# Pooled attention and a gelu layer on one core: v pooled over 128 partitions, its last pools moved by matmuls, and the first batch and the loads put in a new order

## The chip, the cores and the metric

The kernel runs on one core of one Trainium2 chip. The metric is the device time of one launch in microseconds (us), the median of several runs. The profile's own span of an execution is some 1.8 us shorter than the time that is reported for it. Each run has a state: slow when it is over 1.5% above the fastest of the same kernel, otherwise fast. All runs that are compared here ran in the fast state; the one execution that did not is named where it occurs.

## The reference, cut to what matters

Keys and values are averaged over 8 neighbouring positions, 576 positions to 72 pools. Attention goes to these 72 pools, and a two-layer network with a gelu follows. There are 8 batches of 8 heads with 64 columns each.

```python
k_p = k.reshape(B, H, Sp, pool, D).mean(axis=3)     # B 8, H 8, Sp 72, pool 8, D 64
v_p = v.reshape(B, H, Sp, pool, D).mean(axis=3)
scores = scale * np.matmul(q, k_p.transpose(0, 1, 3, 2))
attn = softmax(scores)                              # written out in the original
x = np.matmul(attn, v_p)                            # as 4608 tokens x 512
h = x @ w_in                                        # 512 x 2048
out = gelu_tanh(h) @ w_out                          # 2048 x 512
```

Inputs and output are f32; the kernel multiplies in bf16.

## The kernel before

The 4608 tokens are worked through in 9 groups of 512. Each group has a first phase (64 matmuls with w_in, then gelu on ScalarE) and a second phase (64 matmuls with w_out). The attention of batch g+1 is woven into the second phase of group g. The attention of batch 0 has nothing to hide behind and runs first.

v is put on 72 partitions, one for each pool. It is loaded in 64 partitions and 8 partitions where SyncE issues it:

```python
def load_v(b, eng, h0=0, h1=H):
    ...
    rows = v[b, h0:h1].rearrange("h (j l) d -> j h (l d)", l=8)
    for j0, j1 in ((0, 64), (64, Sp)) if eng is nc.sync else ((0, Sp),):
        eng.dma_start(out=vs[b][j0:j1, h0:h1], in_=rows[j0:j1])
```

k is put on 128 partitions of 4 pools each, and the 64 pools that are left over fill half of a fifth column (`KR`). Pooling is three halving adds on VectorE. The loads are issued in this order: k, v, q of batch 0; two quarters of w_in; k and q of batch 1; two more quarters of w_in; w_out; and v of batch 1 by SyncE in the middle of batch 0's attention.

Batch 0 runs head pair by head pair, and the first 16 matmuls of the first phase are split: their left 288 columns are done inside batch 0's attention.

```python
early = [(fo, ko) for ko in range(KO) for fo in range(4)]
take = (0, 0, 0, 0, 0, 4, 6, 6)
for i, (c, pr) in enumerate(ORDER):
    bank = (4, 6, 0, 2, 4, 6, 4, 6)[i]
    av(0, c, pr, bank)       # outputs and denominators
    norm(0, c, pr, bank)     # Ln, Exp of -1 times it: the inverse
    mult(0, c, pr, bank)
    if i == 3:
        ...
        load_v(1, nc.sync)
    for fo, ko in early[:take[i]]:
        p1_mm(0, fo, ko, 0, CH)
    early = early[take[i]:]
```

PE (TensorE, which does the matmuls) also runs "spins", matmuls on a tile of zeros, where it would stand still. A value matmul below is one that multiplies the exponentials with the pooled v.

The softmax here doesn't subtract the row's maximum and nothing guards it: scores larger than these inputs give would overflow.

Of the kernel before, what the change touches and what calls it, by code (L numbers as in the profile page):

```python
# [18 lines left out]
def kernel(  # L19
# [29 lines left out]
    kvp = ctx.enter_context(tc.tile_pool(name="kvp", bufs=2))  # L49
# [12 lines left out]
    vs, qs = {}, {}  # L62
    kts = [consts.tile([128, KR + 1, 512], F32, name=f"kt{i}") for i in range(2)]

    def load_k(b, engs):
        rows = k[b].rearrange("h (j l) d -> (h j) (l d)", l=8)
        main = rows[0:128 * KR].rearrange("(p r) c -> p r c", r=KR)
        n = KR // len(engs)
        for i, eng in enumerate(engs):
            eng.dma_start(out=kts[b % 2][:, i * n:(i + 1) * n], in_=main[:, i * n:(i + 1) * n])  # L70
        engs[-1].dma_start(out=kts[b % 2][64:128, KR], in_=rows[128 * KR:])

    def load_v(b, eng, h0=0, h1=H):
        if b not in vs:
            vs[b] = kvp.tile([Sp, H, 512], F32, name="vt")
        rows = v[b, h0:h1].rearrange("h (j l) d -> j h (l d)", l=8)

        for j0, j1 in ((0, 64), (64, Sp)) if eng is nc.sync else ((0, Sp),):
            eng.dma_start(out=vs[b][j0:j1, h0:h1], in_=rows[j0:j1])
# [8 lines left out]
    w_in_b = consts.tile([128, KO, DF], BF16, name="w_in_b")  # L88
    w_out_b = consts.tile([128, FO, DM], BF16, name="w_out_b")
    w_in_v = moe_w_in.rearrange("(ko p) f -> p ko f", p=128)  # L90
    w_out_v = moe_w_out.rearrange("(fo p) d -> p fo d", p=128)
# [4 lines left out]
    load_v(0, nc.sync, 0, 4)  # L96
    load_v(0, nc.sync, 4, 8)
# [4 lines left out]
    def load_w_in(i):  # L102
        nc.gpsimd.dma_start(out=w_in_b[:, :, i * 512:(i + 1) * 512], in_=w_in_v[:, :, i * 512:(i + 1) * 512])  # L103

    load_w_in(0)
    load_w_in(1)

# [3 lines left out]
    kTs = [consts.tile([128, 2, H, Sp], BF16, name=f"kT{i}") for i in range(2)]  # L111
    kps = [consts.tile([128, KR + 2, D], BF16, name=f"kp{i}") for i in range(2)]

    vps = [consts.tile([Sp, PR, 2, 2, D], BF16, name=f"vp{i}") for i in range(2)]

    vz = consts.tile([Sp, PR, 2, 2, D], BF16, name="vz")
    ones = consts.tile([Sp, 2, 2, D], BF16, name="ones")
    gate = consts.tile([1, 2], BF16, name="gate")
    idle = consts.tile([128, 512], BF16, name="idle")
    nc.vector.memset(idle, 0.0)  # L120
    nc.vector.memset(kts[0][0:64, KR], 0.0)
    nc.vector.memset(kps[0], 0.0)
    nc.vector.memset(kTs[0], 0.0)
    nc.vector.memset(vz, 0.0)
    nc.vector.memset(ones, 0.0)
    nc.vector.memset(ones[:, 0, 0], 8.0)
    nc.vector.memset(ones[:, 1, 1], 8.0)
    nc.gpsimd.memset(kTs[1], 0.0)  # L128
    nc.gpsimd.memset(kps[1], 0.0)
    nc.gpsimd.memset(kts[1][0:64, KR], 0.0)  # L130
    nc.gpsimd.memset(vps[0], 8.0)  # L131
    nc.gpsimd.memset(vps[1], 8.0)  # L132

    load_k(1, [nc.gpsimd])
    load_q(1)
    load_w_in(2)
    load_w_in(3)
    for i in range(4):
        nc.gpsimd.dma_start(out=w_out_b[:, 4 * i:4 * i + 4, :], in_=w_out_v[:, 4 * i:4 * i + 4, :])
# [7 lines left out]
    def k_steps(b):  # L147

        t = kts[b % 2]
        return [lambda: add(t[:, :, 0:256], t[:, :, 0:256], t[:, :, 256:512]),  # L150
                lambda: add(t[:, :, 0:128], t[:, :, 0:128], t[:, :, 128:256]),
                lambda: add(kps[b % 2][:, 0:KR + 1], t[:, :, 0:64], t[:, :, 64:128])]

    def v_steps(b, hf):
        t = vs[b][:, hf * 4:(hf + 1) * 4]

        def s3():
            w = (vps[b % 2] if b else vz)[:, 2 * hf:2 * hf + 2]
            for e in range(2):
                add(w[:, :, e, e, :], t[:, e::2, 0:64], t[:, e::2, 64:128])  # L160

        return [lambda: add(t[:, :, 0:256], t[:, :, 0:256], t[:, :, 256:512]),
                lambda: add(t[:, :, 0:128], t[:, :, 0:128], t[:, :, 128:256]), s3]
# [4 lines left out]
    def trans_k(b, bank, odd_eng=None):  # L168
        tp = half_bank(bank)[:, 0:(KR + 1) * 128].rearrange("p (r c) -> p r c", c=128)
        kf = kps[b % 2].rearrange("p r d -> p (r d)")  # L170
        for r in range(KR + 1):
            nc.tensor.transpose(out=tp[:, r, :], in_=kf[:, r * D:r * D + 128], identity=identb)  # L172
        tp = tp[0:D]
        n7 = (H - 1) * KH
        for e in range(2):
            copy = nc.scalar.copy if e and odd_eng is nc.scalar else nc.vector.tensor_copy
            o = kTs[b % 2][e * 64:(e + 1) * 64, e]
            copy(out=o[:, 0:H - 1].rearrange("p h (j r) -> p h j r", r=KR),  # L178
                 in_=tp[:, 0:KR, 0:n7].rearrange("p r (h j) -> p h j r", j=KH))
            copy(out=o[:, H - 1, 0:(128 - n7) * KR].rearrange("p (j r) -> p j r", r=KR),  # L180
                 in_=tp[:, 0:KR, n7:128].rearrange("p r j -> p j r"))
            copy(out=o[:, H - 1, (128 - n7) * KR:], in_=tp[:, KR, 64:128])

    def trans_q(b, i, t0, n, bank, eng):
        if b not in qTs:
            qTs[b] = bp.tile([128, 2, TP, 128], BF16, name="qT")
        tp = half_bank(bank)[:, 0:n * 128].rearrange("p (t c) -> p t c", c=128)
        for x in range(n):
            nc.tensor.transpose(out=half_bank(bank)[:, x * 128:(x + 1) * 128],
                                in_=qs[b][:, i, (t0 + x) * 128:(t0 + x + 1) * 128],  # L190
                                identity=identb)
        o = qTs[b][:, i, t0:t0 + n]
        if eng is nc.scalar:
            nc.scalar.copy(out=o, in_=tp)
        else:
            nc.vector.tensor_copy(out=o, in_=tp)

# [9 lines left out]

    def qk(b, c, pr, bank):
        for e in range(2):
            h = 2 * pr + e  # L210
            nc.tensor.matmul(out=PS[:Sp, bank + e, :CH].rearrange("j (t p) -> j t p", p=32),  # L211
                             lhsT=kTs[b % 2][:, c, h, :],
# [3 lines left out]
    def expo(b, c, pr, bank):  # L216
        e = ep.tile([Sp, 2, CH], BF16, name="e", bufs=8)
        nc.scalar.activation(out=e, in_=PS[:Sp, bank:bank + 2, :CH], func=ACT.Exp, scale=1.0 / 64.0)  # L218
        es[b, c, pr] = e

    def flat(w):
        return w.rearrange("j a d -> j (a d)")

    def av(b, c, pr, bank):



        e = es.pop((b, c, pr))
        for x in range(2):
            if b:  # L230
                nc.tensor.matmul(out=PS[:, bank + x, :CH], lhsT=flat(vps[b % 2][:, pr, x]),  # L231
                                 rhs=e[:, x, :], start=True, stop=True)
            else:
                for y in range(2):
                    w = vz[:, pr, y] if x else ones[:, y]
                    nc.tensor.matmul(out=PS[:, bank + 1 - x, :CH], lhsT=flat(w), rhs=e[:, y, :],
                                     start=(y == 0), stop=(y == 1))
# [3 lines left out]
    def norm(b, c, pr, bank):  # L241
        ld = ep.tile([128, CH], F32, name="ld")
        if b:
            nc.scalar.activation(out=ld[0:64], in_=PS[64:128, bank, :CH], func=ACT.Ln)  # L244
            nc.scalar.activation(out=ld[64:128], in_=PS[0:64, bank + 1, :CH], func=ACT.Ln)  # L245
        else:
            nc.scalar.activation(out=ld, in_=PS[:, bank + 1, :CH], func=ACT.Ln)
# [4 lines left out]
    def mult(b, c, pr, bank):  # L252
        rc = rcs.pop((b, c, pr))
        col = b * S + c * CH
        for x in range(2 if b else 1):
            rows = slice(x * 64, (x + 1) * 64) if b else slice(0, 128)
            nc.vector.tensor_tensor(out=xT[rows, pr, col:col + CH], in0=PS[rows, bank + x, :CH],  # L257
                                    in1=rc[rows], op=ALU.mult)

# [9 lines left out]
    def h_bank(g, fo):  # L269
        x, y = x_bank(g), 1 - x_bank(g)  # L270
        if fo == 4:
# [8 lines left out]
    def p1_mm(g, fo, ko, c0=0, c1=GROUP):  # L280
        r0 = g * GROUP
        nc.tensor.matmul(out=PS[:, h_bank(g, fo), c0:c1], lhsT=w_in_b[:, ko, fo * 128:(fo + 1) * 128],  # L282
# [22 lines left out]
    act_set(EXP_SET)  # L305
    for s in k_steps(0):
        s()

    def spin(n):

        for _ in range(n):
            nc.tensor.matmul(out=PS[:, 7, :], lhsT=idle[:, 0:128], rhs=idle, start=True, stop=True)  # L312

    def scores(b, c, pr, bank):
        qk(b, c, pr, bank)
        expo(b, c, pr, bank)

    spin(16)
    trans_q(0, *QG[0], 5, nc.scalar)
    trans_q(0, *QG[1], 6, nc.scalar)  # L320
    spin(4)
    trans_k(0, 4, nc.scalar)
    trans_q(0, *QG[2], 5, nc.vector)
    trans_q(0, *QG[3], 6, nc.vector)
    spin(2)
    for i, (c, pr) in enumerate(((0, 0), (0, 1), (1, 0), (1, 1), (0, 2), (0, 3), (1, 2), (1, 3))):
        if i:
            spin(1)
        scores(0, c, pr, (2, 0)[i % 2])
    for hf in range(2):  # L330
        for s in v_steps(0, hf):
            s()

    early = [(fo, ko) for ko in range(KO) for fo in range(4)]
    take = (0, 0, 0, 0, 0, 4, 6, 6)
    for i, (c, pr) in enumerate(ORDER):
        bank = (4, 6, 0, 2, 4, 6, 4, 6)[i]
        av(0, c, pr, bank)
        norm(0, c, pr, bank)
        mult(0, c, pr, bank)  # L340
        if i == 3:

            vs[1] = kvp.tile([Sp, H, 512], F32, name="vt")
            nc.vector.memset(vs[1][:, 0, 0:1], 0.0)
            load_v(1, nc.sync)
        for fo, ko in early[:take[i]]:
            p1_mm(0, fo, ko, 0, CH)
        early = early[take[i]:]


    for g in range(NG):
        nb = g + 1 if g + 1 < B else None
        act_set(GELU_SET)
        if g + 2 < B:
# [5 lines left out]
            load_v(g + 2, nc.gpsimd)  # L360
# [3 lines left out]
        if nb is not None:  # L364
            kk = k_steps(nb)
            v0, v1 = v_steps(nb, 0), v_steps(nb, 1)
            tk = [lambda: trans_k(nb, 4)]
            if g:
# [90 lines left out]
```

## Time and profile before

| what | before |
|---|---|
| time | 311.72 us (311.4 to 311.77, 3 runs) |
| span of the profiled execution | 309.86 us |
| PE, ScalarE, VectorE busy | 96%, 71%, 51% |
| first phase of group 0 begins | 20.67 us |
| second phase of group 0 begins | 40.03 us |
| last piece of w_out lands | 46.7 us |
| group 1 begins | 58.33 us |
| one steady group, groups 1 to 6 | 31.99 us |
| group 7 begins, to the end | 59.61 us |

The table is to be read from its end. The last 59.6 us hold no attention, and the six groups before them are almost nothing but matmuls back to back. So the moment at which group 1 begins is the number to watch. Two things lead up to it: batch 0's attention on three engines, and the loads of the weights on the DMA engines.

### The profile page before, as it was taken

How to read it: one execution, taken by the hardware profiler on the slowest of the kernel's cores; microseconds unless marked ns; L12 is line 12 of the kernel's file. 1: busy time of each engine (PE TensorE's matmuls, PEld its weight loads, DVE VectorE, ACT ScalarE, POOL GpSimd, SP SyncE). 2: the span in 40 equal slices, each digit the busy share in tenths (PEclk: the TensorE clock that was granted, in tenths of full speed). 3: DMA queues.
4: the chain of work that ended last, by engine and by line, in shares of the span. 5: the costliest groups of instructions: out<-in, count | busy, mean ns of one | idle time of the engine just before them, and what ended most of it. 6: DMA issues, size and time to landing. Idle time of an engine off the chain costs nothing.

```text
span 309.9 us, 4249 instructions
## 1 busy us (share of the span) xinstructions
PE 296.7 (96%) x1516; PEld 149.5 (48%) x1545; DVE 157.1 (51%) x304; ACT 220.9 (71%) x414; POOL 30.8 (10%) x54
## 2 busy tenths in 40 slices
PE   7788899999999999999999999999999999999994
PEld 2455455444544455445544554455445544444441
DVE  3867536647568455855495358636772640020011
ACT  1597478877997799778987898689868987306500
POOL 8530000300301200030003000200000000000000
PEclk9999999999999999999999999999999999999999
DMA  7999995894895982588358826572101120121022
GB/s 225 232 279 249 178 200 116 266 225 87 258 224 113 237 186 62 112 225 175 85 110 232 185 68 100 166 182 68 41 0 33 49 56 0 36 68 34 2 68 69
DMA packets 32701, 41.05 MB, mean 132 GB/s; under 512 B 17608, under 2 KB 21704, under 8 KB 31784
## 3 DMA queue, kind: packets, MB, share of 16 engines
q0 software_dynamic: 10160, 24.26, 35.4%
q1 hardware_dynamic: 22200, 15.74, 21.8%
q10 hardware_dynamic: 320, 0.79, 0.8%
q8 instruction: 12, 0.20, 0.3%
q14 instruction: 9, 0.07, 0.1%
HBM read 36.70 MB, written 9.44 MB: 149 GB/s over the span
## 4 chain that ended last, share of the span: by engine, by line
PE 83%; DMA 12%; POOL 2%; issue 1%; ACT 0%; DVE 0%; POOLq 0%
PE PS L291 38%; PE PS L282 36%; DMA w_out_b<-in_moe_w_out_dram 8%; DMA kt<-in_k_dram 4%; PE PS L211 4%; PE PS L231 4%; PE PS L172 1%; POOL w_in_b L103 0%; POOL kT L128 0%; POOL qb L84 0%; POOL vp L131 0%; POOL vp L132 0%; DVE osb L296 0%; ACT e L218 0%; POOL kt L130 0%
## 5 line engine op out<-in xcount | busy, mean ns | idle before, releaser
L291 PE MATMUL PS<-w_out_b,gT 128*128 128x512 bf16 x560 | 133.8, 379 | 0.9
L282 PE MATMUL PS<-xT,w_in_b 128*128 128x512 bf16 (+2 forms) x580 | 128.3, 373 | 1.8 <-DMA w_in_b<-in_moe_w_in_dram 0.9
L288 ACT ACTIVATE gT<-PS 128x512 bf16<-128x512 f32 x144 | 81.3, 603 | 48.4 <-PE PS L282 48.2
L282 PEld LDWEIGHTS <-w_in_b 128*128 128x128 bf16 x592 | 57.2, 98 | 66.4 <-issue 2.0
L291 PEld LDWEIGHTS <-gT 128*128 128x128 bf16 x576 | 56.0, 97 | 57.1 <-issue 0.8
L296 DVE COPY osb<-PS 128x512 f32<-128x512 f32 x36 | 24.9, 692 | 94.9 <-PE PS L291 94.9
L257 DVE TENSOR_TENSOR xT<-PS,rc 64x288 bf16<-64x288 f32 (+1 forms) x120 | 54.6, 455 | 29.9 <-ACT rc L249 22.3
L218 ACT ACTIVATE e<-PS 72x576 bf16<-72x576 f32 x64 | 40.7, 644 | 8.4 <-PE PS L211 7.6
L145 DVE TENSOR_TENSOR vt<-vt 72x1024 f32<-72x1024 f32 (+1 forms) x32 | 30.5, 952 | 7.0 <-DMA vt<-in_v_dram 6.2
L249 ACT ACTIVATE rc<-ld 128x288 f32<-128x288 f32 x64 | 28.3, 443 | 2.1
L211 PE MATMUL PS<-qT,kT 128*72 128x288 bf16 x128 | 26.1, 286 | 0.4 <-ACT e L218 0.3
L244 ACT ACTIVATE ld<-PS 64x288 f32<-64x288 f32 x56 | 22.8, 408 | 1.4
L245 ACT ACTIVATE ld<-PS 64x288 f32<-64x288 f32 x56 | 22.5, 402 | 1.4
L263 ACT ACT_TABLE_LOAD x17 | 21.8, 1283 | 2.1 <-issue 1.8
L231 PE MATMUL PS<-e,vp 72*128 72x288 bf16 x112 | 23.1, 285 | 0.0
L211 PEld LDWEIGHTS <-kT 128*72 128x72 bf16 x128 | 14.4, 113 | 14.2 <-issue 1.4
L145 DVE TENSOR_TENSOR kt<-kt 128x1280 f32<-128x1280 f32 (+1 forms) x16 | 18.5, 1158 | 4.7 <-DMA kt<-in_k_dram 4.3
L358 POOL COPY gate<-qT 1x2 bf16<-1x2 bf16 x6 | 1.1, 176 | 155.8 <-DMA qT<-qb 155.8
L178 DVE COPY kT<-PS 64x504 bf16<-64x504 bf16 x15 | 10.1, 675 | 7.1 <-PE PS L172 7.0
L231 PEld LDWEIGHTS <-vp 72*128 72x128 bf16 x112 | 11.0, 98 | 3.3
L312 PE MATMUL PS<-idle 128*128 128x512 bf16 x28 | 9.6, 467 | 1.2 <-DVE idle L120 1.2
L145 DVE TENSOR_TENSOR vp<-vt 72x128 bf16<-72x128 f32 x28 | 6.9, 284 | 0.6
(45 smaller groups left out, 75.5 us busy)
## 6 DMA issues: line engine op xcount, KB each, us to landing
out_dram<-osb SPq DMA_DIRECT2D x142, 64.0 KB, 1.7
kt<-in_k_dram POOLq DMA_DIRECT2D x7, 1024.0 KB, 5.8
vt<-in_v_dram POOLq DMA_DIRECT2D x6, 1152.0 KB, 12.4
qb<-in_q_dram POOLq DMA_DIRECT2D x7, 576.0 KB, 15.1
w_in_b<-in_moe_w_in_dram POOLq DMA_DIRECT2D x4, 512.0 KB, 18.4
w_out_b<-in_moe_w_out_dram POOLq DMA_DIRECT2D x4, 512.0 KB, 25.0
vt<-in_v_dram SPq DMA_DIRECT2D x2, 512.0 KB, 11.1
vt<-in_v_dram SPq DMA_DIRECT2D x1, 1024.0 KB, 11.6
```

Source lines behind the costliest of these rows:

```text
L145: nc.vector.tensor_tensor(out=o, in0=a, in1=b, op=ALU.add)
L211: nc.tensor.matmul(out=PS[:Sp, bank + e, :CH].rearrange("j (t p) -> j t p", p=32), lhsT=kTs[b % 2][:, c, h, :], rhs=qTs[b][:, h // 4, :, h ...
L218: nc.scalar.activation(out=e, in_=PS[:Sp, bank:bank + 2, :CH], func=ACT.Exp, scale=1.0 / 64.0)
L231: nc.tensor.matmul(out=PS[:, bank + x, :CH], lhsT=flat(vps[b % 2][:, pr, x]), rhs=e[:, x, :], start=True, stop=True)
L244: nc.scalar.activation(out=ld[0:64], in_=PS[64:128, bank, :CH], func=ACT.Ln)
L245: nc.scalar.activation(out=ld[64:128], in_=PS[0:64, bank + 1, :CH], func=ACT.Ln)
L249: nc.scalar.activation(out=rc, in_=ld, func=ACT.Exp, scale=-1.0)
L257: nc.vector.tensor_tensor(out=xT[rows, pr, col:col + CH], in0=PS[rows, bank + x, :CH], in1=rc[rows], op=ALU.mult)
L282: nc.tensor.matmul(out=PS[:, h_bank(g, fo), c0:c1], lhsT=w_in_b[:, ko, fo * 128:(fo + 1) * 128], rhs=xT[:, ko, r0 + c0:r0 + c1], start=(ko ...
L288: nc.scalar.activation(out=gTs[g][:, fo, :], in_=PS[:, h_bank(g, fo), :], func=ACT.Gelu_apprx_tanh)
L291: nc.tensor.matmul(out=PS[:, o_bank(g, r), :], lhsT=gTs[g][:, fo, r * 128:(r + 1) * 128], rhs=w_out_b[:, fo, :], start=(fo == 0), stop=(fo ...
L296: nc.vector.tensor_copy(out=osb, in_=PS[:, o_bank(g, r), :])
```

## The change

The intent has four parts. v is pooled over all 128 partitions: pools 0 to 63 of heads 0 to 3 lie on the lower 64 partitions and those of heads 4 to 7 on the upper. The last 8 pools of every head go into the half of k's fifth column that was empty. Pooled, they sit on the wrong partitions there and have to be moved. In batch 0 eight matmuls with columns of the identity move them, in later batches a small DMA does. In batch 0 the denominators, which need no v, come ahead of the outputs. And all loads stand in the order in which they are needed. With this comes a layout of w_out in longer rows, for which PE reads w_in's columns with a stride of 4; it gained little: w_out's pieces land 2.49, 2.46 and 2.45 us apart, and 2.48, 2.54 and 2.54 us before. A load of w_in's columns into PE as weights took 113 ns in the mean with the stride and 98 ns without, and 64 matmuls late in the run took 13.81 us in both kernels.

```diff
+        engs[0].dma_start(out=kts[b % 2][64:128, KR], in_=rows[128 * KR:])
+        rows = v[b].rearrange("h (j l) d -> j h (l d)", l=8)
+        for i in range(2):
+            engs[-1].dma_start(out=kts[b % 2][32 * i:32 * i + 32, KR], in_=rows[64:, 4 * i:4 * i + 4])
+    def load_v(b, engs):
+        rows = v[b].rearrange("h (j l) d -> j h (l d)", l=8)
+        for i in range(2):
+            engs[i % len(engs)].dma_start(out=vts[b % 2][64 * i:64 * i + 64], in_=rows[0:64, 4 * i:4 * i + 4])
# ... loads: w_in in two halves, ahead of batch 1; v of batch 1 by GpSimd
     load_w_in(0)
     load_w_in(1)
+    load_k(1, [nc.gpsimd])
+    load_q(1)
+    load_v(1, [nc.gpsimd])
+    for i in range(4):
+        nc.gpsimd.dma_start(out=w_out_b[:, 4 * i:4 * i + 4, :].rearrange("p j d -> p (j d)"), in_=w_out_v[:, i])
# ... the move of the last pools, batch 0 by PE, later batches by DMA
+    for h in range(H):
+        i = h // 4
+        nc.tensor.matmul(out=PS[64 - 64 * i:72 - 64 * i, 7, h * D:(h + 1) * D],
+                         lhsT=identb[0:64, 32 * i + h % 4:32 * i + 32:4], rhs=kps[0][0:64, KR],
+                         start=True, stop=True)
+    def v_moves(b):
+        for i in range(2):
+            nc.sync.dma_start(out=vps[b % 2][64 - 64 * i:72 - 64 * i, 4 * i:4 * i + 4, 0],
+                              in_=kps[b % 2][32 * i:32 * i + 32, KR])
# ... batch 0: denominators of two head pairs, one Ln and one Exp for both, outputs later
+    den0(1, 2, 6)
+    inverse0(1, 2, 6)
+    spin(3, 4)
+    av0(0, 2, 4)
+    mult0(0, 2, 4)
+    spin(3, 0)
+    av0(1, 2, 0)
+    mult0(1, 2, 0)
# ... no part of group 0 is done early; the order of a later group's first 16 matmuls
-            first = [(fo, ko, 0) for ko in range(2) for fo in rest]
-            first += [(late, 0, 0), (late, 1, 0)]
-            first += [(fo, ko, 0) for ko in (2, 3) for fo in rest + [late]]
+            first = [(fo, ko) for ko in range(3) for fo in rest]
+            first += [(late, ko) for ko in range(3)]
+            first += [(fo, 3) for fo in rest + [late]]
# ... weights read with a stride of 4 columns, so that w_out loads in long rows
+        q, j = divmod(fo % 8, 4)
+        nc.tensor.matmul(out=PS[:, h_bank(g, fo), c0:c1], lhsT=w_in_b[fo // 8][:, ko, q * 512 + j:(q + 1) * 512:4],
```

## The prediction

> **What bounds the kernel now.** I read the page first (busy shares, then the rows of slices), then the timeline from the back, to see how much of the span is a fixed stream of matmuls, then the timeline of the first 60 us, and last the windows and the chain, for what the DMA does there.
>
> ```profile
> PE 296.7 (96%) x1516; PEld 149.5 (48%) x1545; DVE 157.1 (51%) x304; ACT 220.9 (71%) x414; POOL 30.8 (10%) x54
> ...
> PE   7788899999999999999999999999999999999994
> ```
>
> PE is the bound; the only slices under nine tenths are the first five (39 us) and the last. From the timeline, PE's matmuls late in the run and at the borders of the first group:
>
> ```profile
> 20.67 0.29 PE L282 MATMUL PS<-xT,w_in_b 128*128 128x288 bf16 x1
> ...
> 40.03 1.46 PE L291 MATMUL PS<-w_out_b,gT 128*128 128x512 bf16 x6
> ...
> 58.33 3.88 PE L282 MATMUL PS<-xT,w_in_b 128*128 128x512 bf16 x16
> ...
> 250.25 13.98 PE L282 MATMUL PS<-xT,w_in_b 128*128 128x512 bf16 x63
> 264.06 13.98 PE L291 MATMUL PS<-w_out_b,gT 128*128 128x512 bf16 x62
> 277.88 13.98 PE L282 MATMUL PS<-xT,w_in_b 128*128 128x512 bf16 x63
> ```
>
> Two phases of 64 matmuls start 13.81 us apart (264.06 - 250.25), 0.216 us a matmul. Group 1 starts at 58.33 and group 7 at 250.25: six groups with attention take 31.99 us each. Their content is 128 x 0.2158 = 27.62, plus 32 attention matmuls at 0.1223 (timeline, start to start) = 3.91, plus 0.28 for five transposes: 31.81. So at most 0.18 us a group, about 1 us in all, can be had after 58.33. Whatever the change gains must move the start of group 1. Before 58.33, group 0's first phase lasted from 20.67 to 40.03 and its second from 40.03 to 58.33.
>
> ```profile
> 12.91 4.60 ACT L218 ACTIVATE e<-PS 72x576 bf16<-72x576 f32 x8 [0.46 <-PE PS L211]
> ...
> 18.86 0.50 PE L236 MATMUL PS<-e,vz 72*128 72x288 bf16 x2 [0.81 <-DVE vz L145]
> ...
> 24.34 0.46 DVE L257 TENSOR_TENSOR xT<-PS,rc 128x288 bf16<-128x288 f32 x1 [0.85 <-ACT rc L249]
> ...
> 27.73 0.44 PE L172 MATMUL PS<-identb,kp 128*128 128x128 bf16 x5 [0.96 <-DVE kp L145]
> ...
> 32.01 1.04 PE L282 MATMUL PS<-xT,w_in_b 128*128 128x512 bf16 x4 [0.52 <-DMA w_in_b<-in_moe_w_in_dram]
> ...
> 36.57 3.63 PE L282 MATMUL PS<-xT,w_in_b 128*128 128x512 bf16 x16 [0.43 <-DMA w_in_b<-in_moe_w_in_dram]
> ```
>
> Batch 0's attention runs from the first exponential at 12.91 to the last product at 24.80. Inside the first phase PE then stands still three times: for k of batch 1 (start-to-start gap 26.39 to 27.73), and for the third and fourth quarter of w_in. The windows show why the weights are late:
>
> ```profile
> 25.00:31.00 6.00, 4.91 (x35) 2.79 (x34) 4.70 (x10) 4.36 (x8) 0.00 (x0) 1.00 1.13 262
> 32.00:35.00 3.00, 2.99 (x21) 1.69 (x22) 0.92 (x2) 1.19 (x2) 0.00 (x0) 1.00 1.61 124
> 36.00:43.00 7.00, 6.57 (x32) 3.08 (x32) 4.23 (x8) 4.92 (x7) 0.00 (x0) 1.00 1.24 207
> ```
>
> The last column is GB/s written. At 36 to 43 only w_out is loading, from f32 to bf16, so 207 written is 414 read. At 32 to 35 it is 124: the tail of v of batch 1 (8 partitions) and weights share the engines, and both crawl.
>
> [...] v of batch 2, 1.18 MB to 72 partitions, was landing from about 60.5 to 68.86, some 140 GB/s, where the k before it (128 partitions) moved at 330 to 350. [...] the k add has mean 1489 ns[...]. [...] no strided weight load is in this trace. A load takes 98 ns here under a 216 ns matmul, so even twice as long it stays hidden.
>
> **The change, part by part.** All loads before w_out's end total 15.4 MB read (3.54 for batch 0, 4.19 w_in, 3.54 batch 1, 4.19 w_out). Before, the last piece landed at 46.7 (chain below), 345 GB/s from 2 us on.
>
> ```profile
> 21.97 24.72 DMA w_out_b<-in_moe_w_out_dram
> ...
> 46.73 0.81 PE PS L291 x3
> ```
>
> (1) Loads. w_in now goes ahead of batch 1, in 2 pieces. With the 8-partition crawls gone, at some 400 GB/s, batch 0 + w_in (7.7 MB) end at about 2.2 + 19.4 = 21.6, landed 22.5. k, q, v of batch 1 follow: k at 25.5, q at 28.5, v (two loads of 64 partitions in series, at half rate, 5 us) at 33.5; w_out's four pieces at about 36, 38.5, 41, 43.5. The two waits for w_in (0.95 us) go.
>
> (2) Start of batch 0. k's adds leave out the mixed column: 1792 elements for 2240, 0.47 us less; its first copies take 4 heads (288 elements for 504). [...] the first exponential needs the first half of q, landed about 9.5, plus a transpose, a 0.45 us copy and the k copy: about 11.0, against 12.91.
>
> (3) ScalarE of batch 0. Eight exponentials stay (8 x 0.645). Ln and Exp go from 8 + 8 of 288 columns (0.39 + 0.44 each, 6.7 us) to 4 + 4 of 576 (about 0.65 each, 5.2 us). That makes 10.4 us: from 11.0 the last inverse ends at about 21.5 with little stall.
>
> (4) VectorE of batch 0, from 11.0: mixed column 0.75; upper copies of k 2 x 0.85; moved v pools 0.7; q copies 0.9; v adds at 128 partitions x 4 heads, 2.6 (two halves of 1.94 + 0.49 before, 4.9); 6.65 in all, so v is pooled at about 18. Then four products of 576 columns (0.75 each), held by ScalarE.
>
> (5) PE of batch 0. After v is pooled: denominators and outputs at 8 x 0.25, three spin groups of 0.65. The first phase's first matmul comes when the product of (1,0) is written, about 20.5, and PE reaches it at 22 to 23. I take 22.5. No part of group 0 is done early any more, so this is LATER than 20.67.
>
> (6) First phase of group 0: 64 x 0.216 + 23 transposes, 1.3: 15.1 us, to 37.6, against 40.03. Batch 1's q copies and v adds end at about 38.4 and 41 on VectorE. They are needed at 39 and 41; I add 0.3. w_out's last piece is needed at 37.8 + 24 x 0.216 + 1.2 = 44.2 and lands at 43.5: no wait.
>
> (7) Second phase: 17.75 us by content (18.30 before). Group 1 starts at about 55.8, 2.5 us sooner than 58.33.
>
> (8) Steady groups: VectorE saves 2 us a group on v and gives back 0.5 on k's six copies, off the path. Earlier last products may save 0.05 us a group: 0.3 in all.
>
> Sum: 311.7 - 2.5 - 0.3 = 308.9; as (5) has more ways to slip than to gain, I say 309.2.
>
> **Rivals.** (a) The first phase starts much sooner, at 20, because the spins only fill waits: 307. For it: they are fillers between waits; against: my VectorE sum has v pooled only at 18. (b) The new start is tangled: k in six copies, PE transposes behind spins, v behind three queues; the first phase starts at 25: 311.7, no gain. For it: the old version overlapped 32 partial matmuls with attention, the new one starts nothing before (1,0). (c) The new move of v pools by SP stalls the value matmuls in steady groups. There SP issues q's transpose first:
>
> ```profile
> 68.86 1.94 DVE L145 TENSOR_TENSOR vt<-vt 72x1024 f32<-72x1024 f32 x2 [4.37 <-DMA vt<-in_v_dram]
> ...
> 72.11 2.68 SPq L200 DMA_TRANSPOSE qT<-qb  x1
> ```
>
> At the old pace the move would go out at 75 and land at 77, while group 1's first value matmuls stand at 76: up to 2 us in that group. With v loaded in 5 instead of 8 us the transpose goes out about 66, so I expect no wait; else 311. In later groups q lands earlier still in the group. (d) w_out still lands at 46.7: 2.5 us lost, 311.5.
>
> **Range and chances.** Over 2% needs 305.4, group 1 starting at 52: the first phase from 19 without a wait. Against it stand ScalarE's 10.4 us. Losing 2% needs 6 us of new waits. So: faster 0.04, same 0.93, slower 0.03; range 306.8 to 311.9.
>
> **What would show it.** In the changed profile: first exponential near 11; first w_in matmul 22 to 23; no wait for w_in; first w_out matmul near 37.7; last w_out piece by 44; group 1 at 55 to 56.5; group 1 to group 7 still 191 to 192 us. It is wrong if the first phase starts outside 20.5 to 24.5, if value matmuls wait for the move, or if group period leaves 31.8 to 32.1.

## The result, and the profile after

The changed kernel takes 308.81 us (median of 4 runs, 308.29 to 309.59) against 311.75 us (311.4 to 311.92, 4 runs) of the kernel before in the same rounds. The ratio is 0.9909, with a 95% interval of 0.9884 to 0.9934. It is faster by about 0.9%, which counts as the same at a threshold of 2%. The outputs are right. A ratio here is the mean time of one kernel's fast runs over that of the other's of the same rounds, so it is not quite the ratio of the medians quoted.

The page of the changed kernel, engines' busy time and PE's row of 40 slices (one slice is 7.7 us):

```profile
PE 298.2 (97%) x1518; PEld 157.4 (51%) x1548; DVE 150.4 (49%) x334; ACT 219.0 (71%) x402; POOL 36.3 (12%) x69
...
PE   8999999999999999999999999999999999999994
```

Four of the five slices that were under nine tenths have filled up. PE's busy time is nearly unchanged (298.2 for 296.7), so the gain is idle time of PE that went. PE's timeline at the borders of group 0 (start, length, engine, line, operation, number of instructions):

```profile
22.08 11.17 PE L336 MATMUL PS<-xT,w_in_b 128*128 128x512 bf16 x50
...
37.18 1.46 PE L345 MATMUL PS<-w_out_b,gT 128*128 128x512 bf16 x6
...
55.62 4.70 PE L336 MATMUL PS<-xT,w_in_b 128*128 128x512 bf16 x20
```

and the same view late in the run:

```profile
246.66 13.98 PE L336 MATMUL PS<-xT,w_in_b 128*128 128x512 bf16 x63
260.47 13.98 PE L345 MATMUL PS<-w_out_b,gT 128*128 128x512 bf16 x63
```

The first phase starts 1.41 us later than before (22.08 for 20.67), and then runs without a wait for weights: 50 matmuls in one row, where the kernel before shows rows of 4 and 16 with waits for w_in ahead of them. It takes 15.10 us instead of 19.36; the 19.36 have a part of batch 0's attention in them. Group 1 begins 2.71 us sooner. From 55.62 to 246.66 it is 191.04 us for six groups, against 191.92. In sums, before to after in the two profiled executions: start of group 1 -2.71, six steady groups -0.88, the last 59.8 us +0.22 (all of it after the last matmul, which in both ends 55.42 us after the start of group 7), together -3.37 us of span. The medians differ by 2.94. The profiled execution of the changed kernel was the fastest of its four.

How batch 0's attention now ends, from the timeline of the first 26 us:

```profile
10.29 2.56 ACT L247 ACTIVATE e<-PS 72x576 bf16<-72x576 f32 x4 [0.49 <-PE PS L239]
...
17.18 0.66 PE L304 MATMUL PS<-e,vz 72*128 72x288 bf16 x4 [0.17 <-DVE vz L139]
...
20.94 0.81 PE L362 MATMUL PS<-idle 128*128 128x512 bf16 x3
...
22.35 0.76 DVE L308 TENSOR_TENSOR xT<-PS,rc 128x576 bf16<-128x576 f32 x1 [0.38 <-PE PS L304]
```

The exponentials begin at 10.29 instead of 12.91. The value matmuls start at 17.18, when the adds of v are done. The last product is written from 22.35 on, beside the first phase, which needs it last. Three spins at 20.94 stand directly ahead of the last values, and so ahead of the first phase.

The windows of the changed kernel (the stretch and its length, then busy time and count of PE, weight loads, VectorE, ScalarE and GpSimd, then PE's clock, DMA share and GB/s written):

```profile
12.00:20.00 8.00, 7.60 (x53) 4.56 (x52) 6.89 (x19) 6.91 (x12) 0.64 (x2) 1.00 1.12 221
...
28.00:33.00 5.00, 5.00 (x25) 2.62 (x24) 3.14 (x4) 3.48 (x7) 0.72 (x2) 1.00 1.06 209
36.00:41.00 5.00, 4.95 (x33) 2.82 (x32) 4.84 (x16) 3.23 (x5) 0.00 (x0) 1.00 1.08 214
```

The crawl of the kernel before (124 GB/s written at 32 to 35) is gone. From 12 to 20 w_in loads, with the end of v of batch 0, at 221 GB/s written. From 36 to 41 only w_out does, at 214; it is halved in width on the way, so that is 428 read. From 28 to 33 the tail of q and the two halves of v land, mostly f32 that is not narrowed, and 209 GB/s written is about half of what w_out reads. The chain that ended last, in the stretch around w_out:

```profile
4.55 21.57 DMA kt<-in_k_dram
...
27.46 16.53 DMA w_out_b<-in_moe_w_out_dram
43.99 0.04 issue
44.03 0.81 PE PS L345 x3
```

The chain goes through the DMA queue up to 43.99, when w_out's last piece lands, and then over to PE. PE's first matmul on that piece could have started at 43.81, so it waited 0.22 us. It had waited as long for the third piece, which landed at 41.55. Without such waits the second phase takes 18.00 us (both runs with v on two queues, below) and not 18.44, so the loads cost 0.44 us here. Attention and loads end almost together, and every experiment below has to be read with both in mind.

### The profile page after: what moved, and what is told of

Read it like the earlier page. It is cut to its first block, busy times and chain, and to the rows that moved or that the text cites. A ratio compares the mean times of both kernels' runs of the same rounds, so it can differ in the third digit from the quotient of the medians.

```text
span 306.5 us, 4325 instructions
## 1 busy us (share of the span) xinstructions
PE 298.2 (97%) x1518; PEld 157.4 (51%) x1548; DVE 150.4 (49%) x334; ACT 219.0 (71%) x402; POOL 36.3 (12%) x69
## 3 DMA queue, kind: packets, MB, share of 16 engines
q0 software_dynamic: 7856, 25.43, 34.9%
## 4 chain that ended last, share of the span: by engine, by line
PE 83%; DMA 12%; POOL 1%; issue 1%; ACT 0%; DVE 0%; POOLq 0%
PE PS L345 38%; PE PS L336 36%; DMA kt<-in_k_dram 7%; DMA w_out_b<-in_moe_w_out_dram 5%; PE PS L239 4%; PE PS L261 4%; PE PS L174 1%; POOL w_in_b L105 0%; POOL qb L86 0%; POOL w_out_b L113 0%; DVE osb L350 0%; ACT e L247 0%; ACT ld L269 0%; ACT ld L268 0%; POOL identb masks.py:199 0%
## 5 line engine op out<-in xcount | busy, mean ns | idle before, releaser
L336 PE MATMUL PS<-xT,w_in_b 128*128 128x512 bf16 x563 | 126.2, 379 | 0.6
L279 DVE TENSOR_TENSOR xT<-PS,rc 64x288 bf16<-64x288 f32 x112 | 51.0, 455 | 31.6 <-ACT rc L271 29.3
L247 ACT ACTIVATE e<-PS 72x576 bf16<-72x576 f32 (+1 forms) x64 | 41.0, 646 | 9.1 <-PE PS L239 8.2
L239 PE MATMUL PS<-qT,kT 128*72 128x288 bf16 (+1 forms) x128 | 25.9, 286 | 0.9 <-ACT qT L214 0.6
L269 ACT ACTIVATE ld<-PS 64x288 f32<-64x288 f32 x56 | 22.5, 402 | 1.3
L261 PE MATMUL PS<-e,vp 72*128 72x288 bf16 (+1 forms) x112 | 23.1, 286 | 0.0
L139 DVE TENSOR_TENSOR kt<-kt 128x1280 f32<-128x1280 f32 (+5 forms) x18 | 18.8, 1044 | 5.5 <-DMA kt<-in_v_dram 2.6
L239 PEld LDWEIGHTS <-kT 128*72 128x72 bf16 (+1 forms) x128 | 13.2, 105 | 15.2 <-DVE qT L216 1.2
L139 DVE TENSOR_TENSOR vt<-vt 128x1024 f32<-128x1024 f32 (+1 forms) x16 | 15.3, 956 | 1.8 <-DMA vt<-in_v_dram 1.5
L184 DVE COPY kT<-PS 64x288 bf16<-64x288 bf16 (+2 forms) x48 | 13.0, 319 | 6.2 <-PE PS L174 6.1
L261 PEld LDWEIGHTS <-vp 72*128 72x128 bf16 (+1 forms) x112 | 11.0, 98 | 3.8
```

The lines of the kernel that those rows point to most:

```text
L139: nc.vector.tensor_tensor(out=o, in0=a, in1=b, op=ALU.add)
L239: nc.tensor.matmul(out=PS[:n, bank + e, :CH].rearrange("j (t p) -> j t p", p=32), lhsT=kTs[b % 2][c][:, h, :n], rhs=qTs[b][:, h // 4, :, h ...
L247: nc.scalar.activation(out=e[:n], in_=PS[:n, bank:bank + 2, :CH], func=ACT.Exp, scale=1.0 / 64.0)
L261: nc.tensor.matmul(out=PS[:, bank + x, :CH], lhsT=window(vps[b % 2][:n], 2 * pr + x), rhs=e[:n, x, :], start=True, stop=True)
L269: nc.scalar.activation(out=ld[64:128], in_=PS[0:64, bank + 1, :CH], func=ACT.Ln)
L279: nc.vector.tensor_tensor(out=xT[rows, pr, col:col + CH], in0=PS[rows, bank + x, :CH], in1=rc[rows], op=ALU.mult)
```

## The experiments

Three sets of four kernels ran, the first on one chip and the other two on another, each set with its own 7 runs of the kernel before: 312.19 us (311.44 to 313.02) for the first four runs told, 311.21 us (310.47 to 312.77) for those with v on two queues, the narrow loads and the old order of w_in as the table has it, and 311.05 us (310.52 to 311.94) for the other four. All runs of this table are in the fast state. The times from the traces are us from the start of the span.

| kernel | us, median | ratio to before | first w_in matmul | first w_out matmul | w_out landed | group 1 |
|---|---|---|---|---|---|---|
| before | 311.75 | | 20.67 | 40.03 | 46.69 | 58.33 |
| after | 308.81 | 0.9909 | 22.08 | 37.18 | 43.99 | 55.62 |
| no late spins | 309.22 | 0.9899 | 21.46 | 37.82 | 45.18 | 56.80 |
| inverses split | 308.58 | 0.9886 | 22.36 | 37.45 | 43.84 | 55.47 |
| move by DMA | 308.98 | 0.9904 | 23.18 | 38.27 | 44.16 | 56.27 |
| old order of w_in | 309.41 | 0.9938 | 22.59 | 38.95 | 44.81 | 56.94 |
| old order, 4 tiles | 309.25 | 0.9944 | 22.34 | 37.59 | 44.96 | 56.59 |
| two narrow loads | 315.81 | 1.0143 | 25.92 | 43.29 | 50.67 | 62.99 |
| v on two queues | 307.94 | 0.9894 | 22.01 | 37.11 | 42.29 | 55.11 |
| the same, no late spins | 307.08 | 0.9863 | 21.25 | 36.34 | 42.06 | 54.34 |
| before, no tails (wrong result) | 310.85 | 0.9997 | 20.04 | 39.16 | 42.35 | 57.18 |
| two queues, no spins, move by DMA | 307.45 | 0.9888 | 21.13 | 36.34 | 42.23 | 54.34 |
| old start of a group | 309.14 | 0.9940 | 22.08 | 37.18 | 44.16 | 55.79 |

In five rows (before, after, no late spins, four tiles, old start of a group) group 1 begins 11.62 to 11.64 us after w_out has landed. That is PE's work from the last piece on, and in these rows the DMA sets group 1. So the 2.71 us that group 1 gains by the change are the 2.70 us by which w_out lands sooner. In most of the others it begins later than that after the landing, and there PE's own work sets it. With the inverses split it is 11.63 us, too, but PE had no wait there: both end together.

### The spins ahead of the last value matmuls

```diff
-    spin(4, 4)
-    spin(3, 6)
-    spin(3, 4)
-    spin(3, 0)
```

> The 13 spins that stand between batch 0's value matmuls in the changed kernel are taken out. Theory A (they lie on PE's path: from 17.2 to 22.1 us PE ran them and the attention matmuls back to back): the first w_in matmul starts about 1.9 us sooner, at 20.2, group 1 at about 53.7 to 54.5 instead of 55.6 (w_out's last piece, landing about 42.5, may take some of it), time 307.0 to 307.8 against 308.8. Theory B (they only fill waits for VectorE and ScalarE): first w_in matmul within 0.5 us of 22.08, time 308.3 to 309.3. Theory C (they keep the clock up): the first matmuls of the phase take twice as long, time 309.5 or more.

Measured: 309.22 us (308.8 to 309.7), ratio 0.9899 with an interval of 0.9865 to 0.9933. The first phase began 0.62 us sooner, although batch 0 started later in this execution. The 22 spins at PE's head take 0.43 us each at first and 0.22 us later. Why is not shown: in the changed kernel's profile the granted clock reads 1.00 in each 2 us from 2 to 8, and the step lies at about 5.4. It differs from execution to execution: here 14 spins were slow, in the changed kernel's profile 10. So the transposes of k behind them began at 9.00 instead of 8.27, though k's adds began at 5.75 (5.80). Counted from these transposes the first matmul with w_in comes after 12.46 us instead of 13.81: the late spins take 1.35 us of PE's path. Theory C did not come: the clock stayed at 1.00 from 16 to 32, and the first 52 matmuls with w_in took 11.38 us. But this line of PE's timeline shows what came next:

```profile
37.82 1.47 PE L345 MATMUL PS<-w_out_b,gT 128*128 128x512 bf16 x6 [1.09 <-DMA w_out_b<-in_moe_w_out_dram]
```

PE waits for w_out's first piece, and again for each of the other three (1.26, 0.52, 0.23 and 0.24 us for the four, from start to start beyond a matmul's own time). So the spins do lie on PE's path, and nothing is gained by taking them out, because w_out is directly behind. Group 1 began at 56.80, later than with them, since w_out itself landed 1.19 us later in this execution. Why is not shown. The four other profiles with the same loads have it between 43.84 and 44.16, so this one stands outside them; but with v on two queues the same edit did not delay it (42.06 for 42.29).

### The inverses merged to 576 columns

```diff
-        nc.scalar.activation(out=ld, in_=PS[:, bank:bank + 2, :CH], func=ACT.Ln)
-        nc.scalar.activation(out=rc, in_=ld, func=ACT.Exp, scale=-1.0)
+        for x in range(2):
+            nc.scalar.activation(out=ld[:, x], in_=PS[:, bank + x, :CH], func=ACT.Ln)
+            nc.scalar.activation(out=rc[:, x], in_=ld[:, x], func=ACT.Exp, scale=-1.0)
```

> Each inverse of batch 0 in two Ln and two Exp of 288 columns in place of one and one of 576: ScalarE has 16 instead of 8 of them, 6.7 us for 5.3. Theory A (ScalarE is not the last to arrive: the last product waited for PE's value matmuls, 0.38 us, not for the inverse): the last inverse ends about 1.0 to 1.4 us later (22.4 to 22.8), the last product 0.1 to 0.6 later, no PE stall over 0.5; group 1 at 55.6 to 56.2, time 308.6 to 309.5. Theory B (merging Ln and Exp is a main part of the gain): group 1 1.4 us later, time 310.2.

Measured: 308.58 us (308.26 to 309.54), ratio 0.9886 (0.9855 to 0.9916); group 1 at 55.47. ScalarE's last inverse ended at 22.04 instead of 21.43. Of these 0.61 us 0.28 are a later start of batch 0 (transposes of k at 8.54 for 8.27), and from there to the first matmul with w_in it is 13.81 us in both. Merging the inverses shortened ScalarE's work and bought no time that these runs show. ScalarE was not on the path that set the end of batch 0.

### The move of the last pools by DMA instead of by matmuls

```diff
-    for h in range(H):
-        ...nc.tensor.matmul(out=PS[64 - 64 * i:72 - 64 * i, 7, h * D:(h + 1) * D], ...)
+    for i in range(2):
+        nc.sync.dma_start(out=vz[64 - 64 * i:72 - 64 * i, 4 * i:4 * i + 4, 0],
+                          in_=kps[0][32 * i:32 * i + 32, KR])
-    for i in range(2):
-        ...nc.vector.tensor_copy(out=vz[p, 4 * i:4 * i + 4, 0], in_=PS[p, 7, ...])
```

> Batch 0's shared pools of v are moved by two small DMAs, as in the later batches, and not by 8 matmuls and two copies. VectorE loses 0.85 us of copies ahead of v's adds, PE 0.3 us. Theory A (the matmul move buys nothing: the pools are ready at 11.3 and needed at 17.2[...]): first value matmul about 0.85 us sooner (16.3), first w_in matmul at 21.2 to 21.6, time 308.0 to 308.6. Theory B (beside the big loads the small DMA is late, over 5.5 us from issue): first value matmul at 17.5 to 20, time 309 to 311.

Measured: 308.98 us (308.71 to 310.67), ratio 0.9904 (0.9867 to 0.9942). The adds of k began at 6.90 instead of 5.80 and the first value matmul at 18.27 instead of 17.18. Both are 1.1 us later, so relative to k's arrival nothing changed, and neither theory held as written. VectorE's timeline shows where the 0.85 us of the two copies went:

```profile
14.25 0.82 DVE L216 COPY qT<-PS 128x640 bf16<-128x640 bf16 x2 [0.87 <-PE PS L204]
```

VectorE then stood 0.87 us waiting for PE's transposes of q, which come before v's adds in its order. This run says nothing yet of how long the DMA itself takes.

### w_in in the old order behind k and q of batch 1

```diff
     load_w_in(0)
     load_w_in(1)          # now quarters of 512 columns
     load_k(1, [nc.gpsimd])
     load_q(1)
+    load_w_in(2)
+    load_w_in(3)
     load_v(1, [nc.gpsimd])
```

> The changed kernel with w_in in four pieces in the old order: two, then k and q of batch 1, then two, then v, then w_out. Theory A (order is worth little; it was the slow v loads that made w_in late before): the third piece lands about 27.5, needed at 29; the fourth about 30.5, needed at 32.5; no wait of PE for w_in over 0.2 us, group 1 at 55.3 to 56.0, time 308.3 to 309.3. Theory B (loads by need is what removed the two waits of 0.95 us): PE waits for w_in again, 0.5 to 1.5 us, group 1 at 56.3 to 57, time 309.5 to 310.3.

The profiled execution took 1673.17 us, in the slow state, and its trace can't be compared. The three timed runs were 309.25, 309.69 and 309.74 us, ratio 0.9912 (0.988 to 0.9944). The same kernel was taken again on the other chip:

> The changed kernel with w_in in four pieces in the old order, once more, as the first profile of it came from an execution of 1673 us that cannot be read beside the others. Theory A (order is worth little): no wait of PE for w_in over 0.2 us, w_out's last piece within 0.6 of 44.0, group 1 at 55.3 to 56.5. Theory B (loads by need removed the waits): PE waits for w_in 0.5 to 1.5 us, group 1 at 56.3 to 57.3.

Measured: 309.41 us (309.2 and 309.62), ratio 0.9938 (0.9888 to 0.9987). PE's timeline has this wait in the first phase:

```profile
30.94 4.29 PE L339 MATMUL PS<-xT,w_in_b 128*128 128x512 bf16 x19 [1.06 <-DMA w_in_b<-in_moe_w_in_dram]
```

That looks like the old wait back again, but the landings say otherwise. The matmul that waits reads columns of the third quarter, which landed at 27.16. The fourth quarter, in the same tile, landed at 30.90. The matmul just before it reads the third quarter too and began at 29.50, so the wait is not one for the whole tile; why it was put on this matmul is not shown. So each quarter was given its own tile:

```diff
-    w_in_b = [consts.tile([128, KO, 1024], BF16, name=f"w_in_b{i}") for i in range(2)]
+    w_in_b = [consts.tile([128, KO, 512], BF16, name=f"w_in_b{i}") for i in range(4)]
-        q, j = divmod(fo % 8, 4)
-        ...lhsT=w_in_b[fo // 8][:, ko, q * 512 + j:(q + 1) * 512:4]
+        j = fo % 4
+        ...lhsT=w_in_b[fo // 4][:, ko, j:512:4]
```

> The changed kernel with w_in in the old order, and each piece in a tile of its own, because in the last run PE waited until the fourth piece had landed for a matmul that reads the third alone. Theory A (order is worth little once each piece is waited for by itself): no wait for w_in over 0.2, group 1 at 55.5 to 56.5. Theory B: a wait of 0.5 or more, group 1 at 56.5 to 57.3.

Measured: 309.25 us (309.24 and 309.27), ratio 0.9944 (0.9921 to 0.9967). No matmul waits for w_in, and the first w_out matmul comes 15.25 us after the first w_in matmul (15.10 in the changed kernel), as w_out's first piece landed only at 37.54. w_out's last piece landed at 44.96 and group 1 began at 56.59, a little outside what was expected of no wait. In the changed kernel and its variants with the same loads, w_out landed between 43.84 and 44.16, and once at 45.18, so these runs don't tell a cost of the old order from the spread of the DMA. The order of w_in by itself is worth some 1 us at most. It is also not needed to remove the two old waits: the kernel before loses them without its 8-partition loads, as is shown below.

### Two narrow loads put back

```diff
+    narrow = consts.tile([128, H, 512], F32, name="narrow")
+    for b in range(2):
+        nc.sync.dma_start(out=narrow[64 + 32 * b:72 + 32 * b],
+                          in_=v[b].rearrange("h (j l) d -> j h (l d)", l=8)[64:])
```

Nothing uses these tiles. They only load what the kernel before loaded on 8 partitions.

> The changed kernel with two loads more, on SP behind v: the 8-partition tails that the kernel before has (128 KB each, to a tile that nobody reads). Theory A (a load to 8 partitions makes all other loads crawl while it lasts): some 2 to 3 us each with under 140 GB/s written, w_out's last piece lands 2 to 3.5 us later (46 to 47.5), PE waits for it, group 1 at 57.6 to 59, time 310.8 to 312. Theory B (it costs its bytes, 0.26 MB or 0.6 us): w_out at 44.6, group 1 at 56.2, time 309.3.

Measured: 315.81 us (315.09 and 316.54), ratio 1.0143 (1.0087 to 1.0199). w_out landed at 50.67, 6.68 us later, and group 1 began 7.37 us later, more than even the theory that these loads are costly expected. The windows show two things:

```profile
13.00:20.00 7.00, 5.04 (x37) 2.87 (x36) 4.94 (x13) 5.26 (x9) 0.00 (x0) 1.00 1.36 148
21.00:23.00 2.00, 2.00 (x8) 0.91 (x7) 0.76 (x1) 0.93 (x2) 0.62 (x1) 0.50 1.12 211
```

For 7 us the DMA writes 148 GB/s where the changed kernel writes 221, with a share of 1.36 for 1.12: the engines are occupied and move less. 0.26 MB more was asked for, and every load behind it came late by far more than that. v's adds end late, PE waits 1.78 us for them, and after that its clock falls to half for a while (0.50 at 21 to 23). It does so again after a wait of 2.11 us for w_out's first piece, from 44.4 to 47.8, in the second phase. This second stretch costs some 1.7 us (an estimate: half of 3.4 us). With it PE's own path ends at 43.29 + 18.00 + 1.7 = 62.99, and w_out's landing alone would have given 50.67 + 11.63 = 62.30. Group 1 began at 62.99, so this is the likely reason that it lost more than w_out did. In the other run the mean clock was 0.997, for 0.988 in this one, and the time 315.09 us, so the loss is not the clock's alone.

### v of batch 1 on two queues at once

```diff
     load_v(0, [nc.sync, nc.scalar])
+    load_v(1, [nc.sync, nc.scalar])
# ...
-    load_v(1, [nc.gpsimd])
```

> The same load of v, spins kept. Theory A: w_out's last piece at 41.5 to 42.5, the 0.2 us wait for it goes, group 1 at 55.0 to 56.0 (PE's own chain, moved by up to 1 us with k's landing), time 308.2 to 309.2. Theory B: as the changed kernel, w_out at 43.7 to 45.

Measured: 307.94 us (307.72 to 308.31), ratio 0.9894 (0.9856 to 0.9932). w_out landed at 42.29, 1.70 us sooner; the runs don't separate the two queues at once from the earlier issue beside w_in's load. Group 1 began at 55.11, only 0.51 sooner, of which 0.44 are the waits for w_out that are gone; the first phase did not begin sooner (22.01). Now PE is the bound alone. Then the spins should count, and they were taken out again as well:

> The changed kernel with v of batch 1 loaded at once on SP and ACT (so that both halves of the partitions are written at the same time, beside w_in) and without the 13 late spins. Theory A (two bounds lie side by side at the start of group 1: PE with its spins, and the landing of w_out's last piece at 44.0, of which v's two halves in series at half rate, 30.3 to 34.9, are 2 us): w_out's last piece lands at 41.5 to 42.5, first w_in matmul at 20.5 to 21.5, no wait for w_out over 0.3, group 1 at 53.8 to 54.6, time 307.0 to 307.8. Theory B (the DMA is bound by bytes, order and width do not matter): w_out's last piece at 43.7 to 45, PE waits for it as without spins alone, group 1 at 55.3 to 56.8, time 308.5 to 309.5.

Measured: 307.08 us (306.73 to 307.5), ratio 0.9863 (0.9831 to 0.9896). The two were taken on one chip in the same rounds, and their ranges don't overlap. The chain that ended last, in the first 56 us, runs through VectorE and PE instead of the DMA:

```profile
15.24 1.24 DVE vt L139
...
17.70 0.67 PE PS L304 x4
...
20.43 0.77 DVE xT L308
21.25 11.38 PE PS L336 x52
```

The first phase starts at 21.25 and group 1 at 54.34. The same edit (no late spins) that gained nothing in the changed kernel gains 0.77 us of group 1 here, because w_out lands 1.9 us sooner (42.06 for 43.99). Of the 1.35 us that the spins take, 0.59 went to a later start, again behind slower spins at the head (transposes of k at 8.79 for 8.20). This version is 1.4% below the kernel before, where the change alone has 0.9%. It did not run in the same rounds as the changed kernel and the two intervals overlap a little (up to 0.9896, from 0.9884), so a lead over it is likely and not shown.

### The kernel before without its 8-partition loads

This kernel gives a wrong result on purpose: the pools 64 to 71 of v of batches 0 and 1 are left out.

```diff
-        for j0, j1 in ((0, 64), (64, Sp)) if eng is nc.sync else ((0, Sp),):
+        for j0, j1 in ((0, 64),) if eng is nc.sync else ((0, Sp),):
-        t = vs[b][:, hf * 4:(hf + 1) * 4]
+        t = vs[b][0:64, hf * 4:(hf + 1) * 4]
```

> The kernel before, its two 8-partition tails of v (batches 0 and 1) not loaded and the v adds on 64 of 72 partitions, so the result is wrong on purpose; everything else stays. Theory A (these tails, not the order of loads, made w_in and w_out late): w_out's last piece lands at 42.5 to 44.5 instead of 46.7, PE's two waits for w_in shrink to under 0.3 in sum, group 1 starts at 55.3 to 57 instead of 58.3, time 309 to 310.5. Theory B (the 0.26 MB alone): w_out at 46.1, group 1 at 57.7, time 311.1.

Measured: 310.85 us (310.12 to 312.02), ratio 0.9997 (0.9964 to 1.0031). The loads do what was hoped: w_out landed at 42.35 instead of 46.69, and both waits for w_in are gone. The windows at 32 to 35, where the kernel before wrote 124 GB/s, and at 22 to 26:

```profile
32.00:35.00 3.00, 3.00 (x22) 1.65 (x21) 1.62 (x4) 1.52 (x3) 0.00 (x0) 1.00 1.24 207
22.00:26.00 4.00, 4.00 (x22) 2.74 (x21) 2.00 (x4) 2.66 (x5) 0.63 (x1) 0.58 1.17 226
```

Yet group 1 began at 57.18, only 1.15 us sooner, with a wait for nothing that loads. PE's own order is the bound then. In this execution PE also ran at half clock from 22.0 to 25.4, which cost some 1.7 us (14 matmuls of 288 columns at 240 ns instead of 122). What made the clock fall is not shown: from 18 to 22 PE was busy for 3.07 us, and in the kernel before for 2.93 us of the same 4, with the clock at 1.00 up to 26. At full clock group 1 would have begun at about 55.5, an estimate. The stretch after the last matmul was 0.62 us longer than before, too. Why the timed runs show no gain at all is not settled: two of the four had clocks of 0.999 and 1.0 and were 310.12 and 310.57 us, no more than 1 us below the median of before. What can be said is that faster loads by themselves did not bring the old kernel the time of the new one. How much of the rest is the new order of batch 0 stays open: no run puts the old order into the changed kernel, and by group 1 it is between nothing (the estimate of 55.5) and 1.6 us (57.18 for 55.62).

### The move by DMA, where VectorE has the time to use it

Built on the version with two queues and without late spins: the pools are moved by the small DMA, the transposes of q come sooner in PE's order, and half of v of batch 1 is issued behind the move.

```diff
+    for i in range(2):
+        nc.sync.dma_start(out=vz[64 - 64 * i:72 - 64 * i, 4 * i:4 * i + 4, 0],
+                          in_=kps[0][32 * i:32 * i + 32, KR])
+    nc.sync.dma_start(out=vts[1][0:64], in_=...)    # v of batch 1, heads 0 to 3
```

> A version that may beat both: no late spins; v of batch 1 half on ACT from the start and half on SP; batch 0's shared pools moved by DMA, and its second q transposes ahead of the denominators, so that VectorE does not wait for them as it did in the run with the move by DMA alone. Theory A: v's adds end 0.6 to 0.9 us sooner than in the version with v on two queues and no spins, first w_in matmul at 20.2 to 21, group 1 at 53.3 to 54.3, time 306.2 to 307.0. Theory B (the small DMA behind v, or w_out's last piece at 42, holds it): group 1 at 54.3 or later, time 307.0 to 308.

Measured: 307.45 us (306.55 to 308.6), ratio 0.9888 (0.9857 to 0.9919). The last of v's adds now ended at 17.09, a microsecond sooner than the 18.09 of the version it is built on. But PE waited:

```profile
17.60 0.65 PE L305 MATMUL PS<-e,vz 72*128 72x288 bf16 x4 [1.37 <-DMA vz<-kp]
```

The two small DMAs were issued at 11.65 and 12.55, and their data was there at 17.6, some 5 us after the second, beside the loads of w_in. Group 1 began at 54.34, exactly as without this edit. So theory B came: the DMA's time took the place of the work that was removed. The edit has more parts than the move (the order of q, where v is issued), and group 1 shows no gain from all of them together. Eight matmuls and two copies of some 0.43 us are no worse in batch 0, where every load is under way.

### The old order of a later group's first matmuls

```diff
-            first = [(fo, ko) for ko in range(3) for fo in rest]
-            first += [(late, ko) for ko in range(3)]
-            first += [(fo, 3) for fo in rest + [late]]
+            first = [(fo, ko) for ko in range(2) for fo in rest]
+            first += [(late, 0), (late, 1)]
+            first += [(fo, ko) for ko in (2, 3) for fo in rest + [late]]
-                    at(min(pos[i] + 9, 62 if i < len(ORDER) else 65), mult, *a)
+                    at(min(pos[i] + 9, 65), mult, *a)
```

> The changed kernel with the old order of the first matmuls of each group and the old place of the product before the last. Theory A (that reordering gave the 0.15 us a group): period of groups 1 to 7 of 31.95 to 32.02 us instead of 31.84, time 308.8 + 0.9 = 309.5 to 309.9. Theory B (it comes from less VectorE work on v): period within 0.03 of 31.84, time as the changed kernel.

Measured: 309.14 us (309.04 and 309.24), ratio 0.9940 (0.9917 to 0.9964). The starts of groups 1 and 7:

```profile
55.79 9.06 PE L336 MATMUL PS<-xT,w_in_b 128*128 128x512 bf16 x39
...
247.63 13.98 PE L336 MATMUL PS<-xT,w_in_b 128*128 128x512 bf16 x63
```

The mean of six groups is 31.973 us, against 31.840 in the changed kernel and 31.987 in the kernel before. The mean hides two kinds of group. In groups 1 to 3 PE pauses twice within 3 us of the group's start, 0.175 and 0.095 us, by their position ahead of the first matmul on the third and on the fourth head pair's products, and these groups take 32.11 us; groups 4 to 6 have no such pause and take 31.84. The kernel before has the same pauses in the same groups (32.12, and 31.86 without), and the changed kernel has none (31.84 in all six). So this reordering, with one product moved two matmuls forward, accounts for 0.80 of the 0.88 us (191.84 for 191.04). The period is what theory A expected; the time is a little under its 309.5, as the kernel before was faster in these rounds, too.

## Why the prediction was right, point by point

The time (309.2 predicted, 308.81 measured), the range and the verdict of the same within 2% all held.

**The bound and where to look.** That all of it had to come from the start of group 1 and only little from the steady groups held: -2.71 and -0.88 of -3.37 us.

**Step (1), loads.** Right in order and nearly in time. w_in landed at 23.03 (22.5 predicted), k of batch 1 at 26.12 (25.5), q at 30.28 (28.5), v at 34.89 (33.5), w_out's pieces at 36.60, 39.09, 41.55 and 43.99 (36, 38.5, 41, 43.5). The two halves of v took 2.03 and 2.58 us, 4.6 us for the 5 that half the rate was to cost. While they landed the DMA wrote 222 and 208 GB/s (30.3 to 32.4 and 32.4 to 34.9), against 428 read for w_out (214 written, 36 to 41). The check of half the rate on the old v was loose: 140 GB/s against 330 to 350 is less than half, and those 72 partitions had the 8 of the tail among them. The step weighed the order of the loads and not their queues; the run with v on two queues, issued early, brought w_out in 1.70 us sooner. The narrow loads were named as the cause of the crawl from a single window. The run that put two of them back, and the one that took them out of the old kernel, show it: w_out's landing moves by 6.68 and by 4.34 us.

**Steps (2) to (5), the start.** The first exponential came at 10.29 (11.0), v was pooled at 17.57 (18), the product of (1,0) was written at 19.69 (20.5), the last inverse ended at 21.43 (21.5), and the first phase began at 22.08 (22.5), later than before as said. The lengths of VectorE's operations in new shapes were the author's estimates. The profiles give 2.37 us for k's first adds instead of 2.84 (0.47 less, as predicted) and about 6.8 us for step (4)'s operations ahead of the products (6.65), of these 2.82 for v's adds (2.6) and 0.98 for the mixed column (0.75). Step (2) counts no wait for the spins at the head, and here there is some luck: the changed kernel has 22 of them, and in six of the eleven profiles of it and its variants the transposes of k waited for these spins and not for k. In the run without late spins the first exponential came at 11.02 for that reason. Step (3) counted ScalarE's saving as part of what set this. The split inverses show that it is not: the last inverse came 0.61 us later (0.33 of it by the split) and nothing followed. The path goes over v's adds on VectorE, the value matmuls and the spins.

**Step (6), first phase.** 15.10 us as predicted, and no wait for w_in. "No wait" for w_out's last piece was off by 0.22 us: it landed 0.5 us later than computed and was needed 0.4 us sooner.

**Step (7), second phase.** 18.44 us for the 17.75 predicted, of which the waits for w_out are 0.44; the rest is small pauses. As the first phase began 0.42 sooner than predicted, the two nearly cancelled, and group 1 came at 55.62 for 55.8. That this came so close is partly luck.

**Step (8), steady groups.** This is the term that was mis-sized: 0.3 us predicted, 0.88 measured. The prediction took the limit of 0.18 us a group from the matmuls' content and the mean of six groups, and then assumed only 0.05 of it. The order of the first 16 matmuls, shown in the diff, was not weighed; the last experiment gives it 0.80, all in groups 1 to 3.

**The rivals.** (a), a first phase at 20 because the spins only fill waits, did not come: v was pooled when the prediction's sum said, and the spins do more than fill waits. Without them the first phase began 0.62 us sooner, which w_out's landing then hid. (b) did not come about; of the 32 partial matmuls that it counts, only the 16 left parts lay inside the old attention. (c) did not either: the transpose of q and the move stand in SyncE's queue like this,

```profile
67.40 2.78 SPq L224 DMA_TRANSPOSE qT<-qb  x1
70.28 1.42 SPq L152 DMA_DIRECT2D vp<-kp  x2
```

4.7 us sooner than the 72.11 of before, and no value matmul waits for it. What it did bring is a wait off the path: the adds of k in group 1 now need v's last pools, too, and they wait 2.62 us for them,

```profile
60.64 2.35 DVE L139 TENSOR_TENSOR kt<-kt 128x1280 f32<-128x1280 f32 x2 [2.62 <-DMA kt<-in_v_dram]
```

which PE doesn't notice. (d), a late w_out, was the nearest miss: it landed 2.7 us sooner than before, and exactly at that moment PE was ready for it. The prediction treated the two bounds one after the other and had a margin of 0.7 us between them. It did not say that any further gain on PE alone would be worth nothing, and that is the main thing that the runs add.

## What to carry to other kernels

When two chains end within a few tenths of a microsecond of each other, as the attention and the weights do here, shorten both in one kernel before judging either edit: removing the spins gained nothing alone and 0.77 us of group 1 once the loads were ahead. Compare the start of a stretch from the same instruction in each profile, not from the start of the span: here the spins at the head made up to 0.8 us of difference between executions. A load that covers few partitions is to be judged by what it does to the loads beside it, not by its bytes: two of 8 partitions, 0.26 MB in all, put w_out 6.68 us later here. Empty space in a wide tile was a good place for it in this kernel. A small DMA in the middle of heavy loads took some 5 us here, and moving a few rows that way on the critical path gained nothing over engines that are at hand.
